# Linear attention and two MLP layers in one kernel: feature projections as pairs of 64-row products

## The chip, the cores and the metric

One core of a Trainium2 chip. The metric is device time in microseconds of one execution; the kernel before took 987.31 us in the median of three runs (986.8 to 987.55). Besides, one execution of it was profiled, and all rows below are from that one.

## What is computed

```python
def _attn_ref(q, k, v, omega):          # q, k, v: 4 x 8 x 576 x 64; omega: 128 x 64
    def phi(x):
        proj = np.einsum('bhsd,md->bhsm', x, omega)
        h = proj - np.sum(x * x, axis=-1, keepdims=True) / 2.0
        h = h - np.max(h, axis=-1, keepdims=True)
        return np.exp(h) / np.sqrt(m)
    q_p, k_p = phi(q * scale), phi(k * scale)
    kv = np.einsum('bhsm,bhsd->bhmd', k_p, v)
    num = np.einsum('bhsm,bhmd->bhsd', q_p, kv)
    den = np.einsum('bhsm,bhm->bhs', q_p, np.sum(k_p, axis=2))[..., None] + 1e-06
    return num / den
def reference(...):
    x = attention output, 2304 x 512
    x = (silu(xn @ w_gate) * (xn @ w_val)) @ w_out      # xn: x normalized by its rms; d_ff 1536
    h = x @ w_in                                        # d_ff 2048
    return (h * sigmoid(h)) @ w2_out
```

The MLP weights come as float64 words, and the kernel decodes them itself.

## The kernel before

**Units.** Attention is cut into units. A full unit is 256 tokens of four heads of `q` or of `k`: each of the 128 partitions holds two neighbouring tokens (r = 0 and 1) of each head, so a head fills 128 columns (r, d). There are 32 full units (16 of keys, 16 of queries) and eight half units for the last 64 tokens of two batches each.

**Steps of a unit.** TensorE transposes the input, one 128x128 block for a head, into one PSUM bank (L629). ScalarE rounds the result to `hl[:, 0]`, and VectorE puts the rest into `hl[:, 1]`, both in a rounded float32 form. Partitions 0 to 63 of `hl` are then the dimensions of token r = 0, and 64 to 127 those of r = 1. `bd` holds the features block-diagonally: rows 0 to 63 give columns 0 to 127, rows 64 to 127 columns 128 to 255, and the rest is zero. A projection (`project`, L658) multiplies one head's block by all of `bd`, 128 rows and 256 columns, in three passes for the two parts (`PASS`). Two heads fill a bank, and a unit has two banks. VectorE takes maxima of each bank (L675) and forms the exponent's bias, and ScalarE takes the exponentials (L700). Key units go on to products with the values (L729), summed over three units; query units are transposed again (L788), multiplied by those sums (L813) and divided (L840). Both L729 and L813 use 64 columns of weights at a time, once for each half of the output's partitions. Then come the norm, a further transpose (L917) and the input `xs` of the MLPs.

**PSUM.** Six banks `b` are shared by all these steps and by the first MLP products; the sums of keys and values have one of their own.

**The order.** Each piece of this work is an `Op` with an engine, an assumed duration, what it depends on, and the buffers that it claims and frees. `ORDER`, a list of numbers, gives the sequence in which all are issued; an engine works through its own in that sequence. The list also holds the first products of the gated MLP (`part`, the first of the L248 products, and `out`, L1037), which stand between pieces of attention once their inputs are there. The assumed durations choose buffers; real waits are semaphores. All else, the sweeps over the two MLPs (L248, L302, L335), follows from about 190 us on and is untouched.

**Weights.** Each weight tile is loaded, decoded by VectorE and GpSimd, and split by ScalarE (L189) and VectorE (L192). The first three tiles of the second sweep take space that the keys' exponentials free (`open_early`, `W_EARLY`).

Of the kernel before, what the change touches and what calls it, by code (L numbers as in the profile page):

```python
# [20 lines left out]
def kernel(  # L21
# [94 lines left out]
    wt = {}  # L116
# [64 lines left out]
    def w_high(job, st):  # L181
        side, slot, key, ap = job
        pool = pools["w"][2] if side and slot < W_EARLY else pools["w"][side]
        t = pool.tile(
            [P, 2 * KC * P + (EDGE if pool is pools["w"][2] and slot == W_EARLY - 1 else 0)], F32R,
            tag=f"w{side}_{slot}", name=f"w{side}_{slot}",
        )
        st.t = t[:, 0:2 * KC * P].rearrange("p (a n) -> p a n", a=2)
        nc.scalar.activation(out=st.t[:, 0, :], in_=st.m.bitcast(F32), func=AF.Copy)  # L189
# [195 lines left out]
    class Op:  # L385
        def __init__(self, kind, eng, dur, emit, deps=(), claim=(), free=(), port=False, xfer=0.0):
            self.eng, self.dur, self.emit, self.xfer = eng, dur, emit, xfer
            self.deps = [d for d in deps if d is not None]
            self.claim, self.free = claim, list(free)
            self.slot, self.end, self.port = {}, None, port or eng == "Pool"  # L390
            self.mode = kind in ("kv", "num")
            ops.append(self)
# [3 lines left out]
    PE_SLOW, TURN, LAND = 5.5, 0.12, 2.4  # L396
# [220 lines left out]
    def add_unit(u):  # L617
# [34 lines left out]
        for r in range(R):  # L652
# [37 lines left out]
            ),  # L690
            [top], free=[(w.sqop, "ns")],
        )
        res = f"et{g}" if kind == "kt" else "e"
        for r in range(R):

            def exps(o, r=r):
# [476 lines left out]
```

## Time and profile before

| | |
|---|---|
| median of three runs | 987.31 us |
| the profiled execution | 987.54 us |
| its span, first to last instruction | 985.8 us |
| TensorE busy | 979.3 us, 99% |
| VectorE, ScalarE, GpSimd busy | 57%, 41%, 30% |
| TensorE's granted clock, mean | 1.00 of full |

The span is the time between the first and the last instruction; 1.74 us of the execution lie outside it. Busy time of TensorE is the union of its records, and these overlap, since a record reaches from the start of a product to the end of its results. What an instruction takes from the engine is read from the distance between starts.

### The profile page before, as it was taken

Reading aid. Unit: us, or ns where it says so; the run is one execution under the profiler, and the core shown is the slowest. Engines: PE = TensorE matmul, PEld = TensorE weight load, DVE = VectorE, ACT = ScalarE, POOL = GpSimd, SP = SyncE. Lnnn points to the kernel's source line nnn. Section 1 sums busy time; section 2 is a strip of 40 time slices with the busy share of each in tenths; the row PEclk is TensorE's granted clock in tenths of the full one; section 3 lists DMA queues with packets and bytes.
Section 4 is the critical chain, followed back from the end, with each engine's and each line's share of the span. In section 5 each row is a group of like instructions: output and inputs, shape, how many; then the busy total and the mean of one; then the engine's idle time right before and its main releaser. Section 6 shows DMA issues by size and latency. Waiting matters only on the chain.

```text
span 985.8 us, 15373 instructions
## 1 busy us (share of the span) xinstructions
PE 979.3 (99%) x6010; PEld 835.4 (85%) x6010; DVE 562.8 (57%) x1168; ACT 400.9 (41%) x922; POOL 294.2 (30%) x308
## 2 busy tenths in 40 slices
PE   9999999999999999999999999999999999999998
PEld 8999988887888888888898888888888888888887
DVE  7998976668633265774234773614634634535633
ACT  6999977753311123341112334443222223222321
POOL 8888664245400022442001322402402312201200
PEclk9999999999999999999999999999999999999999
DMA  7646220123200012221000121201101201100023
GB/s 182 156 115 164 80 63 22 44 65 101 71 21 0 1 43 65 83 89 44 1 1 5 60 65 43 64 22 44 64 22 40 68 22 44 43 1 22 22 86 107
DMA packets 69112, 55.58 MB, mean 56 GB/s; under 512 B 26160, under 2 KB 63280, under 8 KB 69040
## 3 DMA queue, kind: packets, MB, share of 16 engines
q1 hardware_dynamic: 68768, 54.54, 19.0%
q8 instruction: 47, 0.77, 0.3%
q14 instruction: 25, 0.20, 0.1%
q10 hardware_dynamic: 272, 0.07, 0.0%
HBM read 49.87 MB, written 4.72 MB: 55 GB/s over the span
## 4 chain that ended last, share of the span: by engine, by line
PE 94%; DVE 2%; DMA 1%; ACT 1%; issue 0%; POOL 0%; SPq 0%; DVEq 0%
PE g L248 45%; PE y L335 20%; PE y L302 13%; PE b L658 5%; PE b L248 3%; PE b L813 2%; PE kv L729 2%; PE b L1037 2%; PE b L788 2%; PE b L629 2%; PE b L917 1%; DVE w L192 1%; DMA va<-in_v_dram 1%; DVE small L675 0%; DMA raw<-in_moe_w_out_dram 0%
## 5 line engine op out<-in xcount | busy, mean ns | idle before, releaser
L248 PE MATMUL g<-xs,w 128*128 128x512 f32 (+1 forms) x2256 | 469.4, 367 | 0.0
L248 PEld LDWEIGHTS g<-xs,w 128*128 128x128 f32 x2256 | 391.2, 188 | 71.7
L168 POOL TENSOR_TENSOR m<-m,raw 128x512 int32<-128x512 int32 x136 | 189.5, 1393 | 590.6 <-issue 422.3
L242 DVE TENSOR_TENSOR h<-s,h 128x512 fp32r<-128x512 f32 (+1 forms) x134 | 95.8, 715 | 186.2 <-ACT h L241 186.2
L335 PE MATMUL y<-w,h 128*128 128x512 f32 (+1 forms) x870 | 201.0, 388 | 0.0
L335 PEld LDWEIGHTS y<-w,h 128*128 128x128 f32 x870 | 162.2, 188 | 33.3
L241 ACT ACTIVATE h<-s 128x512 fp32r<-128x512 f32 (+1 forms) x134 | 78.7, 588 | 184.2 <-DVE s L271 162.2
L302 PE MATMUL y<-h,w 128*128 128x512 f32 (+1 forms) x648 | 135.6, 366 | 0.5 <-DVE w L192 0.5
L302 PEld LDWEIGHTS y<-h,w 128*128 128x128 f32 x648 | 112.1, 189 | 20.8 <-DVE w L192 0.9
L282 ACT ACTIVATE s<-g 128x512 f32<-128x512 f32 (+1 forms) x80 | 44.5, 556 | 172.1 <-PE g L248 166.9
L346 DVE TENSOR_TENSOR ya<-y,ya 128x512 f32<-128x512 f32 (+1 forms) x91 | 62.2, 684 | 58.0 <-PE y L335 56.7
L271 DVE TENSOR_TENSOR s<-s,g 128x512 f32<-128x512 f32 (+1 forms) x54 | 33.9, 627 | 85.6 <-PE g L248 83.2
L313 DVE TENSOR_TENSOR ya<-y,ya 128x512 f32<-128x512 f32 (+1 forms) x80 | 50.2, 635 | 54.1 <-PE y L302 53.9
L700 ACT ACTIVATE e<-b,nb 128x128 f32<-128x128 f32 x272 | 76.2, 427 | 3.3 <-DVE nb L688 3.1
L189 ACT ACTIVATE w<-m 128x512 fp32r<-128x512 f32 x68 | 43.1, 634 | 68.6 <-POOL m L168 68.1
L658 PE MATMUL b<-bd,hl 128*128 128x256 f32 x432 | 62.3, 289 | 0.6 <-DVE hl L646 0.5
L658 PEld LDWEIGHTS b<-bd,hl 128*128 128x128 f32 x432 | 54.2, 189 | 2.4 <-DVE hl L646 0.7
L192 DVE TENSOR_TENSOR w<-m,w 128x512 fp32r<-128x512 f32 x68 | 54.1, 795 | 2.2 <-ACT w L189 2.2
L675 DVE TENSOR_REDUCE small<-b 128x4 f32<-128x512 f32 x72 | 50.1, 695 | 8.7 <-PE b L658 6.1
L265 ACT ACTIVATE s<-g 128x512 f32<-128x512 f32 (+1 forms) x54 | 29.6, 548 | 58.2 <-PE g L248 58.1
L582 POOL TENSOR_TENSOR sq<-sq 128x256 f32<-128x256 f32 (+1 forms) x80 | 46.5, 589 | 3.2
L578 POOL TENSOR_TENSOR sq<-x 128x512 f32<-128x512 f32 (+1 forms) x40 | 39.5, 992 | 21.8 <-DVE ns L591 13.3
(72 smaller groups left out, 738.0 us busy)
## 6 DMA issues: line engine op xcount, KB each, us to landing
raw<-in_moe_w_out_dram SPq DMA_DIRECT2D x28, 512.0 KB, 3.5
raw<-in_moe_w_in_dram SPq DMA_DIRECT2D x16, 512.0 KB, 3.7
raw<-in_moe_w_gate_dram SPq DMA_DIRECT2D x12, 512.0 KB, 3.5
raw<-in_moe_w_val_dram SPq DMA_DIRECT2D x12, 512.0 KB, 3.5
x<-in_k_dram SPq DMA_DIRECT2D x16, 256.0 KB, 3.6
va<-in_v_dram SPq DMA_DIRECT2D x32, 128.0 KB, 4.2
x<-in_q_dram SPq DMA_DIRECT2D x16, 256.0 KB, 3.2
out_dram<-ya SPq DMA_DIRECT2D x15, 256.0 KB, 2.0
```

The source lines that it names most:

```text
L168: tt(out=mi, in0=mi, in1=(low if step == 5 else high).bitcast(I32), op=ALU.add)
L192: nc.vector.tensor_tensor(out=st.t[:, 1, :], in0=st.m.bitcast(F32), in1=st.t[:, 0, :].bitcast(F32), op=ALU.subtract)
L241: nc.scalar.activation(out=ht[:, 0, :], in_=s, func=AF.Copy)
L242: nc.vector.tensor_tensor(out=ht[:, 1, :], in0=s, in1=ht[:, 0, :].bitcast(F32), op=ALU.subtract)
L248: nc.tensor.matmul(out=ps, lhsT=w[:, a, cc * P:(cc + 1) * P], rhs=xs[j][:, c, cc, :], start=(n == 0), stop=(n == 3 * KC - 1),)
L302: nc.tensor.matmul(out=ps, lhsT=wt[1, "o", f][:, a, d * P:(d + 1) * P], rhs=hs[f][:, c, :], start=(n == 0), stop=(n == nn - 1),)
L313: nc.vector.tensor_tensor(out=y[:, d, :], in0=ps, in1=y[:, d, :], op=ALU.add)
L335: nc.tensor.matmul(out=ps, lhsT=hs[f][:, a, t * P:(t + 1) * P], rhs=wt[2, "p", f][:, c, d0:d1], start=(n == 0), stop=(n == nn - 1),)
L346: nc.vector.tensor_tensor(out=o[:, t, d0:d1], in0=ps, in1=o[:, t, d0:d1], op=ALU.add)
L658: nc.tensor.matmul(out=st.ps[r][:, 2 * j:2 * j + 2, :].rearrange("p h m -> p (h m)"), lhsT=st.hl[:, c, 2 * r + j, :], rhs=bd[:, a, :], sta ...
L675: nc.vector.tensor_reduce(out=st.mx[:, G * r:G * r + G], in_=st.ps[r], axis=AX.X, op=ALU.max)
L700: nc.scalar.activation(out=st.e[r][:, h, :], in_=st.ps[r][:, h, :], func=AF.Exp, bias=st.nb[:, G * r + h:G * r + h + 1],)
```

## The change

In a full unit, `project_rows` takes the place of `project`. It does nothing for the first half and everything for the second: for each head and each pass two products, one with rows 0 to 63 of `hl` and `bd`, one with rows 64 to 127. Each has 128 columns, and the first goes to one bank, the second to the other. So a bank now holds one token row of all four heads, where it held both token rows of two heads. What follows is adapted to that: the maxima wait for both halves, the bias operations read and write through `by_half`, the key products take their pairs in another sequence, the quotients write one token row of four heads, and the sum of squares of a token row waits for its own quotients alone. Half units keep `project`.

The planner gets another duration for the pairs, a third value of `mode`, a few changed durations, empty steps at the end (`late`), and another `ORDER`. The padding of the early weight tiles goes by the sequence in which they are made. A branch for moving exponentials by DMA is added and used for nothing (`BY_DMA` is empty).

```diff
+            def project_rows(o, r=r):
+                st.ps[r] = buf(ps_a, [P, G, P], "b", o.slot["b"])
+                if r == 0:
+                    return
+                for h in range(G):
+                    for n, (a, c) in enumerate(PASS):
+                        for e, rows in enumerate(HALVES):
+                            nc.tensor.matmul(
+                                out=st.ps[e][:, h, :],
+                                lhsT=st.hl[rows, c, h, :],
+                                rhs=bd[rows, a, P * e:P * e + P],
+                                start=(n == 0),
+                                stop=(n == 2),
+                            )
...
-            pj = Op("pj." + kind[0], "PE", 0.73, project, [lo] + bd_ops + pjs, ["b", "pjc"], [(tr, "hl")] if last else [])
+            pj = Op(
+                "pj." + kind[0], "PE", 0.73 if tail else (0.0, PAIRS)[r], project if tail else project_rows,
+                [lo] + bd_ops + pjs, ["b", "pjc"], [(tr, "hl")] if last else [], mode=0 if tail else 2,
+            )
...
-            mxs.append(Op("mx." + kind[0], "DVE", 0.64, maxima, [pj] + mxs, ["nb"] if r == 0 else []))
+            mxs.append(Op("mx." + kind[0], "DVE", 0.64, maxima, pjs + mxs, ["nb"] if r == 0 else []))
...
-                (n // 2, st.e[n // G][:, n % G, :], va.v[:, n // 2, n % 2, :]) for n in range(2 * G)
+                (n % G, st.e[n // G][:, n % G, :], va.v[:, n % G, n // G, :]) for n in range(2 * G)
...
-            if not tail:
-                nc.vector.tensor_tensor(
-                    out=xs_.x[:, :, 2 * hp:2 * hp + 2, :].rearrange("p r h d -> p h r d"),
...
+            nc.vector.tensor_tensor(
+                out=xs_.x[:, half_unit, G * g:G * g + G, :], in0=st.nm[:, :, 0:D],
+                in1=st.rd.to_broadcast([P, G, D]), op=ALU.mult,
+            )
...
-        deps = mults[key]
+        deps = [m for m in mults[key] if m.half_unit == r]
...
     ORDER = [
-        114, 10, 1, 59, 0, 2, 5, 16, 7, 6, 8, 17, 18, 1006, 28, 34, 1007, 1009, 35, 11, 12, 13, 65,
+        10, 59, 0, 114, 1, 16, 17, 1007, 11, 2, 5, 28, 34, 60, 1008, 12, 18, 65, 4, 1009, 6, 7, 8,
...
+        prev = [o for o in ops if o.label in ("xf", "out")] + [xslo[t] for t in range(TB * NE, TB * NE + TB)]
+        for job in prep_list(1)[:W_EARLY]:
+            prev = [Op("late", "PE", 0.227 * 3 * KC, lambda o: None, [*prev, w_done[job[2]]], ["b"])]
+            prev[0].free.append((prev[0], "b"))
```

On TensorE before, in the middle of attention (L658 the projections, L629 and L917 transposes, L729 and L813 the products with 64 columns of weights; a row merges equal instructions that follow each other):

```order
L658 MATMUL b_1850<-bd,hl_1782 128x256 x6
L629 MATMUL b_1863<-ident,x_1635 128x128 x4
L629 MATMUL b_1877<-ident,x_1625 128x128 x2
L729 MATMUL kv_1881<-va_100,e_1731 64x65 x8
L729 MATMUL kv_1881<-va_100,e_1736 64x65 x8
L813 MATMUL b_1904<-kvs_1288,qT_1785 64x65 x8
```

The projections stand next to other 128-row products, and only the products with 64 columns are of another kind.

On TensorE after, at a like place (L678 the pairs, L634, L843 and L963 transposes, L763 and L866 the products with 64 columns of weights); the first row is the last of a block of 24, the last row the first of the next block:

```order
L678 MATMUL b_2193<-bd,hl_2108 128x128
L634 MATMUL b_2223<-ident,x_2167 128x128 x4
L843 MATMUL b_2234<-ident,e_2059 128x128 x4
L963 MATMUL b_2244<-ident,xt_1602 128x128 x4
L866 MATMUL b_2253<-kvs_1504,qT_2048 64x65 x8
L763 MATMUL kv_2117<-va_99,e_2140 64x65 x8
L763 MATMUL kv_2117<-va_99,e_2145 64x65 x8
L763 MATMUL kv_2117<-vat_103,et_2187 64x65 x8
L678 MATMUL b_2305<-bd,hl_2224 128x128
```

A unit's projections are now one block, which here meets 128-row products at one end and follows products with 64 columns at the other; the two banks of a block alternate (`b_2192` and `b_2193` in the first).

## Rows read from the trace of the kernel before

**Rows 1.** The page: span, and TensorE's busy time.
```profile
span 985.8 us, 15373 instructions
...
PE 979.3 (99%) x6010; PEld 835.4 (85%) x6010; DVE 562.8 (57%) x1168; ACT 400.9 (41%) x922; POOL 294.2 (30%) x308
```

**Rows 2.** Waits of TensorE; line, releaser: us in total, times, longest us.
```profile
PE b L1089 <- DVE zero L1065: 1.4, 1, 1.4
PE y L302 <- DVE w L192: 0.5, 1, 0.5
PE b L658 <- DVE hl L646: 0.5, 1, 0.5
```

**Rows 3.** The line of the projections; durations ns min/median/max, first and last start us.
```profile
L658 PEld LDWEIGHTS b<-bd,hl x432: 186/188/192, 7.8 to 176.7; 128*128 128x128 f32 x144
L658 PE MATMUL b<-bd,hl x432: 276/281/388, 8.0 to 176.8; 128*128 128x256 f32 x144
...
  DVE small L675: 6.1, 10
```

**Rows 4.** Busy us of each engine from 20 to 60 us.
```profile
core 0: us, PE busy (x) PEld busy (x) DVE busy (x) ACT busy (x) POOL busy (x), PEclk, DMA share, GB/s
20.00:60.00 40.00, 39.82 (x633) 37.66 (x630) 37.00 (x106) 39.33 (x129) 33.47 (x50) 1.00 0.60 150
```

**Rows 5.** Timeline of TensorE, 24 to 40 us: start, length, instructions.
```profile
30.38 0.64 PE L729 MATMUL kv<-vat,et 128*64 128x65 f32 x16
30.84 1.10 PE L813 MATMUL b<-kvs,qT 128*64 128x65 f32 x32
...
33.84 0.60 PE L629 MATMUL b<-ident,x 128*128 128x128 f32 x4
34.28 0.60 PE L788 MATMUL b<-ident,e 128*128 128x128 f32 x4
34.63 1.62 PE L658 MATMUL b<-bd,hl 128*128 128x256 f32 x12
36.09 0.60 PE L629 MATMUL b<-ident,x 128*128 128x128 f32 x4
```

**Rows 6.** TensorE by form: count, busy us, mean ns.
```profile
L248 PE MATMUL g<-xs,w 128*128 128x512 f32 x1776 | 412.8, 390 | 0.0
```

**Rows 7.** The line of the key and value products; durations as in rows 3.
```profile
L729 PE MATMUL kv<-va,e x512: 219/222/272, 13.8 to 135.9; 128*64 128x65 f32 x171
```

**Rows 8.** Timeline of TensorE, 58 to 64 us.
```profile
60.18 0.38 PE L629 MATMUL b<-ident,x 128*128 128x128 f32 x2
60.49 1.16 PE L729 MATMUL kv<-va,e 128*64 128x65 f32 x32
61.47 0.64 PE L813 MATMUL b<-kvs,qT 128*64 128x65 f32 x16
62.04 1.65 PE L658 MATMUL b<-bd,hl 128*128 128x256 f32 x12
63.53 0.60 PE L788 MATMUL b<-ident,e 128*128 128x128 f32 x4
```

**Rows 9.** Timeline of TensorE, 150 to 175 us.
```profile
163.58 1.58 PE L658 MATMUL b<-bd,hl 128*128 128x256 f32 x12
165.08 1.15 PE L813 MATMUL b<-kvs,qT 128*64 128x65 f32 x32
166.17 1.65 PE L1037 MATMUL b<-h,w 128*128 128x512 f32 x6
167.66 1.53 PE L248 MATMUL b<-xs,w 128*128 128x512 f32 x6
```

**Rows 10.** Timeline of TensorE in a sweep, 300 to 345 us.
```profile
331.92 11.07 PE L248 MATMUL g<-xs,w 128*128 128x512 f32 x48
342.83 2.43 PE L302 MATMUL y<-h,w 128*128 128x512 f32 x10
```

**Rows 11.** VectorE's quotients of four heads by form: count, busy us, mean ns.
```profile
L847 DVE TENSOR_TENSOR xt<-b,rd 128x256 f32<-128x256 f32 x4 | 1.6, 422 | 0.6 <-PE b L917 0.6
```

More of the change, by code (lines that the diff above doesn't have):

```diff
@@ L115 @@
     assert f == NF2
-    wt = {}
+    wt, early = {}, []
     def wcols(w, f):
@@ L184, in w_high @@
         t = pool.tile(
-            [P, 2 * KC * P + (EDGE if pool is pools["w"][2] and slot == W_EARLY - 1 else 0)], F32R,
+            [P, 2 * KC * P + (EDGE if pool is pools["w"][2] and len(early) == W_EARLY - 1 else 0)], F32R,
             tag=f"w{side}_{slot}", name=f"w{side}_{slot}",
         )
+        if pool is pools["w"][2]:
+            early.append(slot)
         st.t = t[:, 0:2 * KC * P].rearrange("p (a n) -> p a n", a=2)
@@ L385, with __init__ @@
     class Op:
-        def __init__(self, kind, eng, dur, emit, deps=(), claim=(), free=(), port=False, xfer=0.0):
+        def __init__(self, kind, eng, dur, emit, deps=(), claim=(), free=(), port=False, xfer=0.0, mode=0):
             self.eng, self.dur, self.emit, self.xfer = eng, dur, emit, xfer
@@ L390, in __init__ @@
             self.slot, self.end, self.port = {}, None, port or eng == "Pool"
-            self.mode = kind in ("kv", "num")
+            self.mode, self.label = 1 if kind in ("kv", "num") else mode, kind
             ops.append(self)
@@ L395 @@
     LAT = {"PE": 0.22, "DVE": 0.15, "ACT": 0.18, "Pool": 0.08, "SP": 0.0}
-    PE_SLOW, TURN, LAND = 5.5, 0.12, 2.4
+    PAIRS = 1.0
+    PE_SLOW, TURN, LAND = 5.5, 0.1, 2.4
     FIRST = {"PE": 1.5, "DVE": 2.0, "ACT": 3.3, "Pool": 2.4, "SP": 0.7}
     ORDER = [
[69 rows of a table removed]
[69 rows of a table added]
     ]
@@ L483, in run_order @@
         slots = {r: [(0.0, None, k) for k in range(n)] for r, n in SLOTS.items()}
-        clock, port, mode, queue = dict(FIRST), 0.0, False, 0.0
+        clock, port, mode, queue = dict(FIRST), 0.0, 0, 0.0
         assert sorted(ORDER) == list(range(len(ops)))
@@ L560 @@
     kv_left, pj_ops, bd_ops, tr_ops = [], [], [], []
+    count, BY_DMA = [0], ()
     def add_load(u):
@@ L623, in add_unit @@
         flat = lambda: w.x.rearrange("p h r d -> p (h r d)")
+        by_half = lambda t: t.rearrange("p (r h) -> p r h", r=R)
         def transposes(o):
@@ L664, in project @@
                         )
+            def project_rows(o, r=r):
[12 more added lines that the diff above has]
+                            )
             last = r == R - 1
-            pj = Op("pj." + kind[0], "PE", 0.73, project, [lo] + bd_ops + pjs, ["b", "pjc"], [(tr, "hl")] if last else [])
+            pj = Op(
+                "pj." + kind[0], "PE", 0.73 if tail else (0.0, PAIRS)[r], project if tail else project_rows,
+                [lo] + bd_ops + pjs, ["b", "pjc"], [(tr, "hl")] if last else [], mode=0 if tail else 2,
+            )
             pjs.append(pj)
+        for r in range(R):
+            last = r == R - 1
             def maxima(o, r=r):
@@ L681, in add_unit @@
             lambda o: nc.vector.scalar_tensor_tensor(
-                out=st.top, in0=w.ns, scalar=half, in1=st.mx, op0=ALU.mult, op1=ALU.add
+                out=by_half(st.top), in0=w.ns.rearrange("p (h r) -> p r h", r=R), scalar=half, in1=by_half(st.mx),
+                op0=ALU.mult, op1=ALU.add,
             ),
@@ L688, in add_unit @@
             lambda o: nc.vector.scalar_tensor_tensor(
-                out=st.nb, in0=w.ns, scalar=half, in1=st.top, op0=ALU.mult, op1=ALU.subtract
+                out=by_half(st.nb), in0=w.ns.rearrange("p (h r) -> p r h", r=R), scalar=half, in1=by_half(st.top),
+                op0=ALU.mult, op1=ALU.subtract,
             ),
@@ L693, in add_unit @@
         res = f"et{g}" if kind == "kt" else "e"
+        base = count[0]
+        if kind[0] == "q":
+            count[0] += R
+        moved = lambda r: kind[0] == "q" and base + r in BY_DMA
         for r in range(R):
@@ L697, in exps @@
                 pool = kp if kind == "kt" else wk
-                st.e[r] = buf(pool, [P, G, M], res, o.slot[res])
+                blocks4 = moved(r)
+                st.e[r] = buf(pool, [P, 4, G, 32] if blocks4 else [P, G, M], res, o.slot[res])
                 for h in range(G):
+                    src = st.ps[r][:, h, :]
                     nc.scalar.activation(
-                        out=st.e[r][:, h, :], in_=st.ps[r][:, h, :], func=AF.Exp,
+                        out=st.e[r][:, :, h, :] if blocks4 else st.e[r][:, h, :],
+                        in_=src.rearrange("p (a f) -> p a f", a=4) if blocks4 else src, func=AF.Exp,
                         bias=st.nb[:, G * r + h:G * r + h + 1],
@@ L711, in add_unit @@
         else:
-            evs = [add_flip_e(st, r, exs[r]) for r in range(R)]
+            evs = [add_flip_e(st, r, exs[r], moved(r)) for r in range(R)]
             num = None
@@ L780, in add_kv, with add_flip_e, move, turn @@
             add_tail(b - 1, g, 1, tst, tex, vop, [(tex, f"et{g}"), (pad, f"vt{g}")])
-    def add_flip_e(st, r, ex):
+    def add_flip_e(st, r, ex, by_dma):
         pe = {}
+        if by_dma:
+            def move(o):
+                pe[0] = buf(wk, [P, G, P], "qT", o.slot["qT"])
+                for a in range(4):
+                    nc.sync.dma_start(
+                        out=pe[0][32 * a:32 * a + 32],
+                        in_=st.e[r][:, a].rearrange("p h f -> p (h f)"),
+                    )
+            def turn(o):
+                turned = st.e[r].rearrange("p a h f -> p (a h f)").rearrange("p (h t) -> p h t", h=G)
+                nc.vector.transpose(
+                    out=turned.rearrange("p h (t b) -> p b h t", b=4),
+                    in_=pe[0].rearrange("p b (h f) -> p b h f", h=G),
+                )
+                st.e[r] = turned
+            mv = Op("ed", "SP", 2.1, move, [ex], ["qT"], xfer=1.5)
+            tp = Op("eT", "DVE", 0.92, turn, [mv], free=[(mv, "qT")])
+            return tp, (ex, "e")
         def flip(o):
@@ L794, in evac @@
             nc.scalar.activation(out=st.e[r], in_=pe[0], func=AF.Copy)
-        return Op("ev", "ACT", 0.495, evac, [fl], ["qT"], [(fl, "b")])
+        ev = Op("ev", "ACT", 0.495, evac, [fl], ["qT"], [(fl, "b")])
+        return ev, (ev, "qT")
     def add_q(u, whole, half_unit, evs, prev):
@@ L800, in add_q @@
         tail = kind == "qt"
-        hp = 2 * g + half_unit
         st = State()
-        ev = evs[half_unit]
         def numerators(o):
@@ L811, in numerators @@
                     else:
-                        rhs = kvfirst[b, g].sb[:, 2 * half_unit + a // 2, :]
+                        rhs = kvfirst[b, g].sb[:, a, :]
                     nc.tensor.matmul(
@@ L815, in numerators @@
                     )
-        deps = evs + [prev, kvcopy[b, g]]
-        free = [(ev, "qT")]
+        deps = [ev for ev, _ in evs] + [prev, kvcopy[b, g]]
+        free = [evs[half_unit][1]]
         if tail:
@@ L838, in quotients @@
                 xs_.x = buf(wk, [P, R, H, D], "xt", o.slot["xt"])
-            if not tail:
-                nc.vector.tensor_tensor(
-                    out=xs_.x[:, :, 2 * hp:2 * hp + 2, :].rearrange("p r h d -> p h r d"),
-                    in0=st.nm[:, :, 0:D].rearrange("p (h r) d -> p h r d", r=2),
-                    in1=st.rd.rearrange("p (h r) o -> p h r o", r=2).to_broadcast([P, 2, 2, D]),
-                    op=ALU.mult,
-                )
-            else:
-                nc.vector.tensor_tensor(
-                    out=xs_.x[:, 0, G * g:G * g + G, :], in0=st.nm[:, :, 0:D],
-                    in1=st.rd.to_broadcast([P, G, D]), op=ALU.mult,
-                )
+            nc.vector.tensor_tensor(
+                out=xs_.x[:, half_unit, G * g:G * g + G, :], in0=st.nm[:, :, 0:D],
+                in1=st.rd.to_broadcast([P, G, D]), op=ALU.mult,
+            )
         mu = Op("mu", "DVE", 0.34, quotients, [rec, None if lead else xs_.op], ["xt"] if lead else [], [(num, "b"), (num, "nmc")])
@@ L855, in add_q @@
         mults.setdefault(key, []).append(mu)
+        mu.half_unit = half_unit
         if len(mults[key]) == (2 if tail else 4):
@@ L950, in add_weight @@
             prev = Op(
-                "w_dec", "DVE", 0.37, lambda o, s=s: w_decode(job, st, s, o.slot.get("wm")), [lop, prev],
+                "w_dec", "DVE", 0.39, lambda o, s=s: w_decode(job, st, s, o.slot.get("wm")), [lop, prev],
                 [] if s else ["wm"], port=True,
@@ L1021, in add_block @@
             hi = Op("h_hi", "ACT", 0.52, high, [s2], ["h"])
-            low[f] = Op("h_lo", "DVE", 0.61, lowp, [hi], free=[(gh, "s")], port=True)
+            low[f] = Op("h_lo", "DVE", 0.65, lowp, [hi], free=[(gh, "s")], port=True)
             hcl.append(hi)
```

136 rows, old and new, of the table ORDER are left out of this document.

## The prediction

> **What bounds the kernel now.** I read the page's busy times and slices first, then the waits of TensorE, then its instructions by form, then single stretches of its timeline, and last the other engines by stage. TensorE is busy 979.3 of 985.8 us [rows 1], and its waits for other engines are short: 1.4 us at the start, and then none over 0.5 [rows 2]. The feature projections lie between 8 and 177 us [rows 3]. In a stretch of that, 20 to 60 us, TensorE is busy 39.8 of 40 us, with ScalarE at 39.3 and VectorE at 37.0 beside it [rows 4]. So the time is the length of TensorE's own stream: what the change takes from it or adds to it moves the end, as long as the other engines keep up. Busy time alone does not show what an instruction costs there, since the records overlap; I therefore take costs from start to start of merged stretches.
>
> **What a projection product costs now.** Four transposes follow four others at 0.44 us (33.84 to 34.28). The next four transposes and twelve products take 1.81 us (34.28 to 36.09), so twelve products take 1.37 and one 0.114 us [rows 5]. A full unit has twelve, and there are 32 full units: 384 of the 432 products of this line [rows 3] (the other 48 belong to the half units, which stay). 384 x 0.114 = 43.8 us.
>
> **What a pair would cost.** The change puts two products of 64 rows and 128 columns in place of one of 128 rows and 256 columns: 384 pairs, 768 instructions, each with a weight load of 128 columns. No row of before shows a 64-row product, so I bound it.
> - The stream: a product of 512 columns is recorded with 390 ns, one of 256 with 281 [rows 3, 6], so 128 columns are worth 0.055 us.
> - The load: the longest record of a projection is 388 ns against a median of 281 [rows 3]. The excess, 0.107 us, is a load of 128 columns that nothing hid. For the products of 64 columns it is 272 against 222, 0.050 us [rows 7]: half the columns, half the load.
> - Side by side: the program's 64-column products leave two records each, and in a running stretch 16 records take 0.46 us (30.38 to 30.84) [rows 5], so two records take 0.0575, which is one 64-column load and 0.0075. Two loads thus run beside each other where the array is used in column halves. That they do so in row halves is what the change needs, and I assume it.
>
> A pair is then its own load, 0.107 + 0.0075 = 0.1145 us, for the load outlasts the stream of 0.055. The bounds: if only the stream counts, 0.055 + 0.0075 = 0.0625; if the next load of a half must wait for its product, 0.107 + 0.055 + 0.0075 = 0.17; if the two loads take turns, 0.222. The unhidden load is the nearest row to what is asked, since it has the same 128 columns, so I take 0.1145. 384 pairs are 44.0 us against 43.8: the halved streaming gains nothing, because the loads that now hide behind 256 columns come to the front.
>
> The excess of 0.107 us for 128 columns and 0.050 for 64 goes with columns; whether it goes with rows no run here shows. The Trainium skill, TensorE: Matmul & The Clock Gate, section "LDWEIGHTS (loading the stationary operand)", says that the load takes columns over 1.2 ns, whatever the rows, which is 0.107 us here: the trace agrees for full rows, and by that rule a 64-row load is no shorter. It speaks against the change.
>
> **What the switching costs.** A stretch of 64-column products stands apart from its neighbours in the timeline. From 60.18 to 63.53 us stand two transposes, 48 records and twelve products [rows 8]. At their running rates (0.109, 0.0575 for two, 0.114) that is 0.22 + 1.38 + 1.37 = 2.97 us; it took 3.35, so going in and out cost 0.38. A second stretch agrees: from 163.58 to 167.66, twelve products, 32 records and six products of 512 columns [rows 9] should be 1.37 + 0.92 + 1.36 (0.227 each, 10.91 us over 48, [rows 10]) = 3.65 and took 4.08, so 0.43. Part is the unhidden load at each end, the rest a drain. I take the lower, 0.38 for in and out, 0.19 for one change. TensorE's order before holds 24 such stretches, so 48 changes. Now the 32 blocks of pairs are a third kind: 42 changes between full and 64-column products, 40 between full and 64-row, 24 between 64-row and 64-column, together 106. 58 more x 0.19 = 11.0 us. That a change to and from row halves costs what one to and from column halves does is not shown; the bounds are 0 (the pairs' loads slip in under the work before) and 0.215 a change, 12.5 us.
>
> What the trace shows at a change is the 0.38 us above. The Trainium skill, TensorEngine Tiling (Array Packing), "Key Properties", says that changing the tiling mode drains the engine, and its "Available Configurations" list 64 rows x 128 columns as a mode of its own. By that rule the blocks of pairs pay at both ends, as summed.
>
> **The other edits.** VectorE, ScalarE, GpSimd and SP issue as many instructions as before. 32 quotients take the shape that four have already, at 422 ns [rows 11]. The two maxima of a unit now wait for both banks, so the first starts up to a block later; behind them on VectorE stand other units' operations, and TensorE has other units' products, as it does now where no wait for them shows [rows 2]. If that cover fails, VectorE's wait for a projection (6.1 us over ten times now [rows 3]) grows, and TensorE waits about as much. The planner's new constants and the empty steps at its end emit nothing; they and the new order can at best remove the one late weight, 0.5 us [rows 2].
>
> **The sum.** The profiled execution took 987.54 us (span 985.8, 1.74 around it). 987.54 + 0.2 + 11.0 - 0.5 = 998.2, and the median of before lies 0.23 lower: 998 us. Its own range: pairs from 0.107 (-2.9 us) to 0.12 (+2.1), changes from 5.5 us (half price) to 12.5: 989 to 1002.
>
> **Rivals.**
> 1. The pairs are bound by the stream (faster). A block of 64 rows might load in half the time, or both loads hide in the row half that is not streaming. Pairs of 0.0625 to 0.088 us make 24 to 33.8 us, 10 to 20 less than now, and with 11 us of changes and the late weight gone 977.5 to 987. For it: the two records in 0.0575 us, which show two halves of the array at work at once. Against it: the column halves run exactly at their load. ScalarE limits it as well, 39.3 of 40 us busy from 20 to 60 us [rows 4]. By the rows a load of 128 columns lasts twice as long as their stream. Break-even is at 0.087 us a pair. Chance 0.31, around 981. The Trainium skill, TensorE: Matmul & The Clock Gate, "Part 3: Packing small matmuls — row/col tiling", has row tiles start about 4 ns apart, and four of them gain 3.07 times at 512 columns; by that rule alone this rival holds, but no run here shows it, nor 128 columns there.
> 2. The halves do not overlap (much slower). At 0.17 us a pair +21.3, at 0.222 +41.4, plus 10.5: 1019 or 1039. It decides from 0.13 us a pair on. For it: nothing here shows row halves together. Against: column halves do it. Chance 0.11.
> 3. The pairs cost as forecast and the changes nothing: 0.2 - 0.5 leaves 987, no change. Against it: both stretches above. Chance 0.08.
> 4. The forecast, 998: 0.50.
>
> About 0.2%, 2 us, can be told from no change. Faster by more: rival 1 without its upper end, and a little of 3, 0.31. Within: 0.08. Slower: forecast, rival 2 and the rest of 3, 0.61. Range 978 to 1003: it holds the forecast's own range, rival 3 and most of rival 1, and leaves out rival 2 and the fastest end.
>
> **What would show it.** Right: from one pair to the next 0.107 to 0.12 us, the two records of a pair some ns apart, 64-row loads recorded about as long as now (188 ns), a block of 24 about 1.4 us in itself and 1.7 with its two ends, TensorE without new waits, and the extra time all before 200 us, the sweeps after it unchanged. Wrong: pairs at 0.06 to 0.09 us, loads of some 135 ns, or a block that starts right behind its neighbours; and for rival 2 the two products one after the other. A wait of TensorE for VectorE's maxima, or for ScalarE, would be a cost that I left out.

## The result, and the profile after

The changed kernel takes 996.51 us (median of 4 runs, 995.23 to 997.7) against 987.09 in the same measurement: 1.0094 times as long, 95% interval [1.0082, 1.0107]. 998 us had been forecast, in a range of 978 to 1003. The profiled execution took 995.89 us, 8.35 more than that of before. Where the 8 us are, and whether for the reasons given, is read from these rows.

The page: span, and busy time of the engines [rows 1].

```profile
span 993.8 us, 16155 instructions
...
PE 985.2 (99%) x6394; PEld 836.4 (84%) x6394; DVE 565.3 (57%) x1168; ACT 401.3 (40%) x922; POOL 292.7 (29%) x308
```

TensorE is 8.6 us of its span short of always busy, where before it was 6.5: the engine still sets the time. The line of the pairs, with durations in ns as minimum, median, maximum, and VectorE's waits for it [rows 3, 7]:

```profile
L678 PEld LDWEIGHTS b<-bd,hl x768: 182/188/188, 8.4 to 175.0; 64*128 64x128 f32 x192
L678 PE MATMUL b<-bd,hl x768: 268/272/327, 8.4 to 175.1; 64*128 64x128 f32 x192
...
  DVE small L700: 11.0, 15
```

A load of 64 rows and 128 columns is recorded with 188 ns, as a load of 128 rows was. Half the rows, the same load. The timeline, with a block and its neighbours [rows 5, 8]:

```profile
95.22 0.60 PE L843 MATMUL b<-ident,e 128*128 128x128 f32 x4
95.75 1.55 PE L678 MATMUL b<-bd,hl 64*128 64x128 f32 x24
97.24 0.66 PE L634 MATMUL b<-ident,x 128*128 128x128 f32 x4
...
109.50 1.10 PE L763 MATMUL kv<-va,e 128*64 128x65 f32 x32
110.53 0.66 PE L634 MATMUL b<-ident,x 128*128 128x128 f32 x4
111.03 0.60 PE L843 MATMUL b<-ident,e 128*128 128x128 f32 x4
111.56 1.55 PE L678 MATMUL b<-bd,hl 64*128 64x128 f32 x24
113.04 1.66 PE L250 MATMUL b<-xs,w 128*128 128x512 f32 x6
```

A block of 24 products, twelve pairs, takes 1.49 us from its start to that of what follows (95.75 to 97.24, and 1.48 from 111.56 to 113.04). The ends cost outside the block too: the four transposes before a block take 0.53 us (95.22 to 95.75, 111.03 to 111.56), where four before other transposes took 0.44 [rows 5]; four transposes behind 64-column products take 0.50 (110.53 to 111.03). Before, four transposes and twelve whole products took 1.81 us together [rows 5], 0.35 and 1.46 by their starts; now four transposes and twelve pairs take 2.02.

The waits of TensorE, all but the two shortest [rows 2]:

```profile
PE b L1135 <- DVE zero L1111: 1.4, 1, 1.4
PE b L843 <- DVE xt L892: 0.9, 1, 0.9
PE b L634 <- DMA x<-in_k_dram: 0.6, 1, 0.6
PE b L678 <- ACT e L733: 0.6, 1, 0.6
PE y L304 <- DVE w L194: 0.6, 1, 0.6
PE b L663 <- DVE hl L651: 0.4, 1, 0.4
PE b L678 <- ACT qT L849: 0.3, 1, 0.3
```

Some are new: without the first and the late weight (L304) the view lists 3.2 us, 2.8 of them in these rows, where that of before lists 1.0 (0.5 in [rows 2] and two shorter ones). And the late weight stayed, at 0.6.

Where the time was lost: the first 256-column products of the sweeps (a run of 36) start here:

```profile
211.48 5.75 PE L248 MATMUL g<-xs,w 128*128 128x256 f32 x36
```
```profile
221.18 5.75 PE L250 MATMUL g<-xs,w 128*128 128x256 f32 x36
```

The first row is of before, the second of after: 9.7 us were lost by then, all ahead of the sweeps. From there to the end of the span the sweeps took 772.6 us where they had taken 774.3, so 1.7 us came back. That is not the scatter of an execution: in the traces of this section and the next, the two kernels with the old `ORDER` show 774.2 and 774.3 us for this part, and the eleven with the new code and orders 772.5 to 772.7. Nearly all of it lies in the L248 products of 512 columns; what makes them shorter is not shown, since order and placement of buffers changed together. 9.7 less 1.7 leaves 8.0 us, by which the spans differ; 0.35 us lie outside them.

### The profile page after: what moved, and what is told of

It is laid out like the page before. It is cut to its first block, busy times and chain, and to the rows that moved or that the text cites. A ratio compares the mean times of both kernels' runs of the same rounds, so it can differ in the third digit from the quotient of the medians.

```text
span 993.8 us, 16155 instructions
## 1 busy us (share of the span) xinstructions
PE 985.2 (99%) x6394; PEld 836.4 (84%) x6394; DVE 565.3 (57%) x1168; ACT 401.3 (40%) x922; POOL 292.7 (29%) x308
## 4 chain that ended last, share of the span: by engine, by line
PE 95%; DVE 3%; ACT 1%; DMA 1%; issue 0%; POOL 0%; DVEq 0%; ACTq 0%
PE g L250 44%; PE y L337 20%; PE y L304 12%; PE b L678 5%; PE b L250 3%; PE kv L763 2%; PE b L866 2%; PE b L1083 2%; PE b L843 2%; PE b L634 2%; PE b L963 1%; DVE w L194 1%; PE b L663 1%; DVE m L154 0%; DVE small L700 0%
## 5 line engine op out<-in xcount | busy, mean ns | idle before, releaser
L304 PE MATMUL y<-h,w 128*128 128x512 f32 (+1 forms) x648 | 135.6, 366 | 0.6 <-DVE w L194 0.6
L304 PEld LDWEIGHTS y<-h,w 128*128 128x128 f32 x648 | 112.1, 189 | 20.8 <-DVE w L194 1.0
L678 PE MATMUL b<-bd,hl 64*128 64x128 f32 x768 | 51.4, 276 | 1.1 <-ACT e L733 0.6
L678 PEld LDWEIGHTS b<-bd,hl 64*128 64x128 f32 x768 | 46.4, 187 | 7.0 <-issue 2.6
```

The costliest lines, as they stand in the source:

```text
L304: nc.tensor.matmul(out=ps, lhsT=wt[1, "o", f][:, a, d * P:(d + 1) * P], rhs=hs[f][:, c, :], start=(n == 0), stop=(n == nn - 1),)
L678: nc.tensor.matmul(out=st.ps[e][:, h, :], lhsT=st.hl[rows, c, h, :], rhs=bd[rows, a, P * e:P * e + P], start=(n == 0), stop=(n == 2),)
```

## The experiments

The theory to test is the prediction's: a pair lasts as long as its load, so nothing is won, and the changes between kinds of tile are the loss. Rivals are the other order, the stream (64-row products that stream slowly), and halves that wait for each other. A further rival, that the number of instructions sets a pair, has a row against it: the 64-column products start two records in 0.0575 us [rows 5], about twice as fast as pairs do.

**1. Whole products at the pairs' place.** The order stays, and the block is again twelve products of 128 rows.

```diff
-                    for n, (a, c) in enumerate(PASS):
-                        for e, rows in enumerate(HALVES):
-                            nc.tensor.matmul(out=st.ps[e][:, h, :], lhsT=st.hl[rows, c, h, :], ...
+                    for n, (a, c) in enumerate(PASS):
+                        nc.tensor.matmul(out=st.ps[h // 2][:, 2 * (h % 2):2 * (h % 2) + 2, :]..., lhsT=st.hl[:, c, h, :], rhs=bd[:, a, :], ...
```

(What depends on the banks' contents goes back too; steps that the order has ahead of what they now need are put off until it is there.)

> The changed kernel with its order, but the twelve products of a full unit are again 128 rows by 256 columns, in one block where the pairs stood. Theory (changes of mode cost the time, a pair costs what a whole product does): only the changes to and from 64-column products are left, so 6.5 to 11 us go and about 1 us comes from 384 products at 0.1145 instead of 0.112: 986 to 991 us. Rival (the other order and its waits cost the time): 994 to 998 us, as the changed kernel.

Measured: 990.7 us (990.13 to 991.27), 1.0036 [1.0023, 1.0049] times before. So 5.8 us of the loss go with the pairs. The first 256-column products of its sweeps start here:

```profile
216.30 5.75 PE L250 MATMUL g<-xs,w 128*128 128x256 f32 x36
```

By then it has lost 4.8 of the 9.7 us; its sweeps give back the same 1.7. The 4.8 us go with the other order: it has 33 separate stretches of 64-column products where the old one has 24, 18 changes more, and 18 x 0.19 us, the price that the prediction read off such stretches, is 3.4. Its waits, counted as above, are 1.5 us against 1.0, and some 0.9 us stay without a cause shown. The order was thus a part of the loss, for the most part by the same price.

**2. Half the stream, the same load.** Each product is cut into two of 64 columns of the features.

```diff
+                    for f in range(2):
...
-                                out=st.ps[e][:, h, :],
+                                out=st.ps[e][:, h, 64 * f:64 * f + 64],
-                                rhs=bd[rows, a, P * e:P * e + P],
+                                rhs=bd[rows, a, P * e + 64 * f:P * e + 64 * f + 64],
```

> The changed kernel with each 64-row product cut into two of 64 columns of the features: 24 pairs a unit, each with the same load of 128 columns and half the stream. If the load sets a pair (0.107 to 0.112 us whatever the stream): 24 x 0.112, 1.34 us more a unit, about 1039 us. If the stream sets it (128 columns in 0.109 us, as long as a transpose's): pairs of 0.055 to 0.06, the block as long as now, 994 to 1000 us.

Measured: 1055.19 us, one run. It lies above both numbers, and the granted clock of TensorE was below full in several stretches up to 140 us. Busy time of each engine, in us, by stretches:

```profile
core 0: us, PE busy (x) PEld busy (x) DVE busy (x) ACT busy (x) POOL busy (x), PEclk, DMA share, GB/s
20.00:30.00 10.00, 10.00 (x101) 9.42 (x101) 2.76 (x8) 1.42 (x5) 3.11 (x5) 0.50 0.11 32
40.00:44.00 4.00, 4.00 (x82) 3.89 (x81) 2.86 (x8) 2.78 (x9) 2.27 (x5) 1.00 0.26 74
100.00:120.00 20.00, 19.91 (x269) 18.27 (x267) 12.12 (x39) 11.61 (x35) 8.61 (x14) 0.76 0.37 91
140.00:180.00 40.00, 40.00 (x622) 36.34 (x620) 27.33 (x73) 27.91 (x80) 19.46 (x26) 1.00 0.27 69
```

The clock was 0.50 of full from 20 to 30 us, which is 1.2 GHz, while the engine was recorded as busy all the time. So the total can't be compared with the forecasts, and the test is a block at the full clock. In the timeline, the first row is a block at the low clock, the second one at the full clock, with what follows it:

```profile
24.17 5.33 PE L679 MATMUL b<-bd,hl 64*128 64x64 f32 x48
40.93 2.87 PE L679 MATMUL b<-bd,hl 64*128 64x64 f32 x48
43.73 0.66 PE L844 MATMUL b<-ident,e 128*128 128x128 f32 x4
```

24 pairs take 2.80 us, and in the trace each pair starts about 0.112 us after the one before it. Half the stream, and the pair as long as with 128 columns. So the stream does not set a pair; the load, the same in both, does.

**3. Twice the stream.** 256 columns in each 64-row product; half of them are zeros and overwrite a neighbour's place, so the projections are not the reference's.

```diff
-                                out=st.ps[e][:, h, :],
+                                out=st.ps[e][:, 2 * (h // 2):2 * (h // 2) + 2, :].rearrange("p h m -> p (h m)"),
-                                rhs=bd[rows, a, P * e:P * e + P],
+                                rhs=bd[rows, a, :],
```

> The changed kernel with 256 columns in each 64-row product (the other half of the block-diagonal columns, zeros, comes along and writes over a neighbour's place, so the projections are not the reference's). If the load sets a pair and 256 columns stream at the rate of whole products: 0.115 us a pair, 996 to 999 us. If 64-row products stream at half rate: 0.22 us a pair, 1.3 us more a unit, about 1037 us.

Measured: 998.11 us, one run. Its timeline and the records of its line:

```profile
36.97 1.68 PE L678 MATMUL b<-bd,hl 64*128 64x256 f32 x24
38.58 1.15 PE L763 MATMUL kv<-va,e 128*64 128x65 f32 x32
```
```profile
L678 PE MATMUL b<-bd,hl x768: 272/277/389, 7.4 to 177.2; 64*128 64x256 f32 x192
```

A block lasts 1.61 us, 0.12 more than with half the columns, and half of that is the longer step from its first pair to the second. From pair to pair the records show 0.117 us in the median, as whole products of 256 columns do in the trace of before (0.117). So 64 rows stream 256 columns at the full rate: the rival of the slow stream falls for this rounded form. With the experiment before: 64, 128 and 256 columns cost 0.112, 0.112 and 0.117 us a pair.

**4. One product more in each block, of either kind.** With 128 rows it adds two changes of mode (changes from one kind of tile to another) to a block, with 64 rows none. Its result is overwritten.

```diff
+                    if h == 1:
+                        nc.tensor.matmul(out=st.ps[1][:, 3, :], lhsT=st.hl[:, 0, 3, :], rhs=bd[:, 0, P:2 * P], start=True, stop=True)
```

(In the second kernel `st.hl[HALVES[1], 0, 3, :]` and `bd[HALVES[1], 0, P:2 * P]`.)

> The changed kernel with one more product of 128 rows and 128 columns in the middle of each block of pairs (its result is overwritten by the fourth head's pair). It adds 32 products and 64 changes of mode, and leaves all else. If a change costs what the trace shows (0.09 us longer at each end, and the first load of either kind not hidden): 0.35 to 0.45 us a unit, 1007 to 1011 us. If changes are free: 32 x 0.11, 1000 us.

> As the run with one more product in the middle of each block, but that product has 64 rows, so no mode changes. If the 12 us of that run are the changes: only what is left of a product of its own, 32 x 0.05 to 0.11, 998 to 1000 us. If a further product in the middle costs them whatever its kind: 1007 to 1011 us.

Measured: 1008.86 us (1007.24 to 1010.47) with 128 rows, 999.18 (999.1 to 999.26) with 64. The difference of 9.7 us over 64 changes is 0.15 us a change, from two executions each: the two profiled ones differ by 8.1, which makes 0.13. The blocks themselves say 0.15. The timelines show one of the first kernel, then one of the second, each with the added product as L686:

```profile
60.84 0.89 PE L678 MATMUL b<-bd,hl 64*128 64x128 f32 x12
61.66 0.33 PE L686 MATMUL b<-bd,hl 128*128 128x128 f32 x1
61.91 0.89 PE L678 MATMUL b<-bd,hl 64*128 64x128 f32 x12
62.73 0.69 PE L871 MATMUL b<-kvs,qT 128*64 128x65 f32 x16
```
```profile
58.14 0.99 PE L678 MATMUL b<-bd,hl 64*128 64x128 f32 x13
58.86 0.27 PE L686 MATMUL b<-bd,hl 64*128 64x128 f32 x1
58.97 0.83 PE L678 MATMUL b<-bd,hl 64*128 64x128 f32 x11
59.73 0.69 PE L871 MATMUL b<-kvs,qT 128*64 128x65 f32 x16
```

Six pairs 0.82, the lone product 0.25, six pairs 0.82 us: 1.89 us, where the block with an added product of 64 rows lasts 1.59 (58.14 to 59.73). Two changes thus cost 0.30 us. The changes are dear, at 0.15 where 0.19 had been taken.

**5. The two halves one after the other.** For each head, the three passes of one row half are issued ahead of the three of the other.

```diff
-                    for n, (a, c) in enumerate(PASS):
-                        for e, rows in enumerate(HALVES):
+                    for e, rows in enumerate(HALVES):
+                        for n, (a, c) in enumerate(PASS):
```

> The changed kernel with the three passes of the upper row half issued before the three of the lower one, for each head; same instructions. If two products run beside each other only where the two halves alternate: most products take a load of their own, 0.107 to 0.112 us, up to 24 x 0.112 a unit, 1025 to 1040 us. If the halves work independently whatever the sequence: 996 us as the changed kernel.

Measured: 996.0 us, one run: nothing lost, as expected for halves that work independently. A block in its timeline:

```profile
95.85 1.56 PE L678 MATMUL b<-bd,hl 64*128 64x128 f32 x24
97.34 0.66 PE L634 MATMUL b<-ident,x 128*128 128x128 f32 x4
```

1.49 us again. In the trace two records start 10 ns apart, then 0.10 us pass, where they were 3 ns apart with halves in turn. So products of the two halves still run beside each other when three of one half are issued ahead of three of the other. The second rival is out: row halves do run beside each other, in either sequence.

**6. Unrounded float32.** If the loads are the price, fewer loads should win. In these kernels full units project unrounded float32 in one pass, so no split into a rounded part and a rest: as pairs, as four tiles of 64 rows and 64 tokens, and, in the kernel before with its order, as whole products.

```diff
-                    for n, (a, c) in enumerate(PASS):
                         for e, rows in enumerate(HALVES):
                             nc.tensor.matmul(
                                 out=st.ps[e][:, h, :],
-                                lhsT=st.hl[rows, c, h, :],
-                                rhs=bd[rows, a, P * e:P * e + P],
+                                lhsT=st.hl[rows, 0, h, :].bitcast(F32),
+                                rhs=bdf[rows, :],
...
```

(Four tiles: `out=st.ps[e][t, h, :]` and `st.hl[rows, 0, h, t]` for `t` in `HALVES`. Whole: `st.hl[:, 0, 2 * r + j, :]` and a block-diagonal `bdf` of 256 columns.)

> Pairs as in the changed kernel, but in unrounded float32 with one pass in place of three: four pairs a unit, each product in two records; the split into a rounded part and a rest is not done for full units. Taken from the 64-column float32 products (0.0575 us for 65 columns in two column halves, so about 0.11 for 128), a pair is 0.11 to 0.22 us, 0.45 to 0.9 us a unit against 1.34 now. Load theory (two loads of 128 columns, 0.107 each, for a product): 0.22 us a pair, 0.46 us a unit or 15 us less than the changed kernel: about 981 us; if float32 loads take half of that, 967. Rival (four passes at half rate): 0.43 us a pair, 1.7 us a unit, 1008 us.

> The kernel before with its order, and each three-pass product of a full unit as one product of unrounded float32, 128 rows by 256 columns, two records each; no new kind of tile, no rounding and rest in full units. If a record is bound by its load (0.107) and streams a column in 0.43 ns: 0.23 us a product, 0.92 us a unit against 1.37, 972 us. If float32 streams at half that rate, as the transposes' 0.109 us for 128 columns suggest: 0.43 us a product, 1.72 us a unit, 998 us.

> Float32 pairs (985 us) with each product cut into two of 64 tokens, so four tiles of 64 rows by 64 columns, each with a load of 64 columns (0.050 us). If the load bounds the float32 pairs: half the time, 0.45 us less a unit, about 971 us. If their stream does (128 columns in 0.107 us): no gain, 984 to 990 us.

Measured: pairs 985.17 us (0.9982 [0.9973, 0.9991] times before), whole products 996.53 (1.0093 [1.0078, 1.0108]), four tiles 984.54 (0.9973 [0.9964, 0.9983]). Timelines of pairs, of whole products and of four tiles, and the loads of the pairs and the records of the four tiles:

```profile
46.09 1.16 PE L680 MATMUL b<-bdf,hl 64*128 64x128 f32 x16
47.19 0.65 PE L635 MATMUL b<-ident,x 128*128 128x128 f32 x4
```
```profile
63.05 1.03 PE L661 MATMUL b<-bdf,hl 128*128 128x256 f32 x4
63.91 0.38 PE L630 MATMUL b<-ident,x 128*128 128x128 f32 x2
```
```profile
46.26 1.10 PE L681 MATMUL b<-bdf,hl 64*64 64x128 f32 x32
47.29 0.66 PE L635 MATMUL b<-ident,x 128*128 128x128 f32 x4
```
```profile
L680 PEld LDWEIGHTS b<-bdf,hl x512: 182/188/188, 7.9 to 164.1; 64*128 64x128 f32 x171
```
```profile
L681 PEld LDWEIGHTS b<-bdf,hl x1024: 129/133/134, 8.0 to 163.4; 64*64 64x64 f32 x171
L681 PE MATMUL b<-bdf,hl x1024: 269/269/322, 8.0 to 163.5; 64*64 64x128 f32 x171
```

A record of whole products streams 256 columns in 0.215 us (four in 0.86), twice as long as a rounded one: here the forecast with the slow stream, 998 us, was right. So 128 columns stream in 0.107 us, as long as a load of 128 columns. The pairs gained 11.3 us on the changed kernel, not the 15 that the load theory gave: a block is 0.39 us shorter (1.10 against 1.49), 12.5 us in 32 units, and TensorE's waits, counted as above, grew from 3.2 to 4.1 us. With four tiles the load is recorded 55 ns shorter than the pairs' (133 against 188), and the block is hardly shorter: 1.03 us, against 1.10 of the pairs. So the load alone did not hold the pairs; load and stream both last about 0.107 us there, and making one shorter gains almost nothing. The total, 984.54 against 985.17, is not clear of the noise.

**7. Another order for the four tiles.** I searched `ORDER` by the kernel's own planner, with 0.92 us for a block and 0.14 for a change, and ran two of the orders found. Nothing else changes.

> The float32 kernel in four tiles (984.5 us) with an order that I searched by the kernel's own planner, with 0.92 us for a block and 0.14 us for a change: 95 changes in place of 106. If changes and waits of TensorE decide: 11 x 0.15 us and some of its 3 to 4 us of waits less, 980 to 983 us. If the planner's picture does not hold on the chip: 984 to 987 us.

> The same with the second order found, 103 changes, its gain in the waits alone by the planner: 981 to 984 us if these go, 984 to 987 us if not.

Measured: 982.16 us (0.9953 [0.9936, 0.9969]) and 982.02 (0.9947 [0.9932, 0.9962]). Both beat the kernel before and the changed one. Against the four tiles in the old order (984.54) the gain is some 2.4 us, at the edge of what the intervals can tell. The longest waits of TensorE in the second:

```profile
PE b L1142 <- DVE zero L1117: 1.4, 1, 1.4
PE b L684 <- ACT e L739: 0.7, 2, 0.6
PE y L305 <- DVE w L195: 0.6, 1, 0.6
PE b L1125 <- DMA om<-in_omega_dram: 0.5, 1, 0.5
PE b L638 <- DMA x<-in_k_dram: 0.5, 1, 0.5
```

None behind the first is over 0.7 us. Counted as above, the waits are 3.2 us in this kernel and 3.8 in the one with 95 changes, where the four tiles in the old order have 4.8. With 0.15 us a change, 3 changes and 1.6 us of waits make 2.1 us, and 11 changes and 1.0 us make 2.7: that 103 and 95 changes give the same time fits changes and waits together.

## Why the prediction was right, point by point

- **TensorE sets the time.** Right: its span is as full as before (8.6 us short of it against 6.5), and the loss is where its stream got longer.
- **A pair costs its load.** Right in mechanism and size: 0.112 us a pair against 0.1145 taken, 188 ns for a load as said. 384 pairs are 43.0 us against 43.8 for whole products: -0.8 us, where +0.2 stood. The 0.114 us for a whole product came from one stretch; over all neighbouring records of that line in before, steps over 0.15 us left out, the mean is 0.116, and by it the pairs save 1.5 us. Experiments 2 and 3 show that it is the load and not the stream. The Trainium skill's rule (TensorE: Matmul & The Clock Gate, "LDWEIGHTS (loading the stationary operand)"), that rows don't shorten a load, is now shown by a row.
- **Changes.** Right in mechanism, mis-sized: 0.15 us a change for row halves against 0.19, by experiment 4. 58 more are 8.7 us, not 11.0, if those of the column kind cost the same. A part of them, 18 of the column kind, comes with the order alone (experiment 1).
- **The other edits hide.** Wrong by 2.8 us: I forecast no new waits and 0.5 us off the late weight. The weight stayed late, and waits of 0.3 to 0.9 us came up, for quotients, an input and exponentials. With the late weight that is 2.3 us more. Which edit brings them I did not test: experiment 1 keeps the order and the block's double claim of banks and has smaller waits, so the order alone does not bring all of them. VectorE's waits for a projection grew as well, from 6.1 us over ten [rows 3] to 11.0 over fifteen; TensorE's list names no wait for maxima, and whether those for exponentials come from there is not shown.
- **The sweeps unchanged.** Wrong by 1.7 us, a gain that the sum did not have. It comes with the new code and order also where the products are whole (experiment 1); its cause stays open.
- **The sum.** -0.8 + 8.7 + 2.3 = 10.2 us by measured terms (9.5 with -1.5 for the pairs), against the 9.7 us lost by the start of the sweep's 256-column products; less the 1.7 us of the sweeps it is 8.5, against 8.35 between the two profiled executions. The forecast had 10.7. That it came out near is partly luck: pairs and changes were taken 1.0 and 2.3 us too dear, and the sweeps' gain of 1.7 us was not seen, while the waits were taken 2.8 us too cheap.
- **Rivals.** The stream as the bound: out, by experiments 2 and 3; rival 1 would have needed pairs under 0.087 us. Halves that don't overlap: out, by experiment 5. Free changes: out, by experiment 4.

## What to carry to other kernels

Before cutting a product into smaller tiles, compare its stream with its load: if the load is hidden behind the stream now and does not shrink with the cut, the cut wins nothing. Then count the changes between kinds of tile and price them from stretches that the trace already has. If loads are the price, fewer passes help more than smaller tiles: one float32 pass in place of three rounded ones turned the same pairs from a loss of 9 us into a gain of 2, and as four tiles with an order searched for them of 5.

## What the runs showed that I had not expected

- The two row halves keep abreast even where three products of one are issued ahead of three of the other: a block of 1.49 us either way (experiment 5).
- A float32 record streams 256 columns in 0.215 us, a rounded one in about 0.117 (experiments 6 and 3): half the rate, in two records a product.
- With 64 columns in a product of 128 weight columns the granted clock fell to 0.50 of full from 20 to 30 us, with TensorE recorded as busy throughout, rose and fell again several times, and was full from 140 us on (experiment 2, a single execution; that the short products are the reason is not shown). Its mean over that execution was 0.977; in the profiled executions of all other kernels here it was 0.999 or 1.
- The sweeps, whose products are the same, are 1.7 us shorter in every kernel with the new code (from 211.48 us of 985.8 before, from 221.18 of 993.8 after).
